# The first pair's keys turned on TensorE, and the 64 last positions in a transfer of their own

## The chip, the core and the metric

The kernel runs on one core of one Trainium2 chip. A time is the device time of one execution in microseconds (us). Where a median is given it is over several executions; the trace belongs to a single profiled one. Sizes are KB of 1024 bytes.

## What is computed

Attention with a decay in place of a softmax ("retention"), then two feed-forward layers. All data is float32.

```python
scores = q @ k.T / 8                      # 4 batches x 8 heads, 576 positions, 64 dims
ret    = scores * D                       # D[i,j] = gamma_h**(i-j) for i >= j, else 0
x      = (ret @ v) as (2304, 512)         # all heads side by side
h      = x @ w_in                         # 512 -> 2048
x      = (h * clip(h+3, 0, 6) / 6) @ w_out
h      = x @ w2_in                        # 512 -> 1024
solu   = h * softmax(h)
out    = (layernorm(solu) * g) @ w2_out   # 1024 -> 512
```

## The kernel before

**Pairs.** The 32 heads are taken two at a time, as 16 pairs (`pr`). The 576 positions of a head are four blocks of 128 and a last one of 64. `load_pair` brings four arrays for a pair: `rk` (k with the 64 dims of the two heads on the 128 partitions, one column per position), `rq` (q in the same way), `rv` (v with positions on the partitions) and `rn` (k again, now with positions, the keys, on the partitions). Before the change `rk`, `rq` and `rv` hold all 576 positions, with the last 64 at their end; `rn` holds 512. The first three pairs (`EARLY`) land in buffers that weights use later and are named `raw`; from the fourth pair on the buffers are `rk`, `rq`, `rv` and `rn` themselves.

**Work on a pair.** `scores` makes on TensorE (PE) the product of keys and queries inside each block (`s`), which ScalarE (ACT) copies out and GpSimd (POOL) masks (`st`). `short` does the same for the last 64 positions (`z`; VectorE, DVE, multiplies it by a mask into `st4`). `prep` scales v (`v`). `chunk_states` multiplies `rn` with `v` (`u`), and DVE sums it up from block to block (`state`). `values` adds st times v to the output `xp`, and the second half of `short` adds `st4` times v and state times q. `evac_x` takes xp out as `xa`, and splits it into the high and low parts of `x`. `places` makes a table once, with one PE product (`place`). From the pair with number 6 on, the first layer's products (`h`, six at a time) stand between the pairs.

**Order of the work.** For pair `pr` the loop puts on PE: scores of `pr`, values of `pr - 1`, short of both, states of `pr`. This order of PE is fixed by the text. The other engines and the DMA queue of SyncE (SP) get their order from `Plan`, which plays the program through with costs of its own and sorts each engine's queue by when an instruction is due. Its constants `HELD` (times at which it takes the transfers to stand still), `DMA_ONE` (the slowest single transfer) and the like change no instruction, only the order. Each queue then works strictly in that order. A transfer carries one of eight semaphores in turn, and the transfer eight places further down SP's queue waits for it: at most eight are under way, and the issue of the n-th tells that the one eight earlier has landed. ACT issues two small ones, which take two of these turns.

**The start.** Ahead of the first scores stand `N_WARM` products of a tile of zeros, `idle` (`warm`), which nobody reads. POOL makes the masks (`mask`).

Every recorded engine instruction has line 67, a helper's, so rows are told apart by the names of tiles. One float32 product shows as two records on PE, so eight products `s` are x16.

Of the kernel before, what the change touches and what calls it, by code (L numbers as in the profile page):

```python
# [109 lines left out]
class Plan:  # L110


    LOOK, HOP, DMA_US, DMA_KB, DMA_ONE = 0.8, 0.2, 2.2, 375.0, 150.0
    DEEP, PASSES, YIELD, GAP, KEEP = 3.0, 5, 0.3, 5.0, 1e9
    HELD = ((3.0, 1.4), (23.0, 0.3))

# [137 lines left out]
    def simulate(self, nexts, free, loose=False):  # L254
# [101 lines left out]
@with_exitstack  # L356
def retention_hardswish_solu_kernel(ctx, tc, kt, qt, kn, vt, w1, w2i, w2o, gln, decay, place, out):

# [536 lines left out]
    idle_b = known("x2e", idle)  # L895
    PA = {"rk": 3, "rq": 4, "rn": 3, "rv": 3, "v": 3, "st0": 2, "st1": 2, "state": 2, "st4": 2, "xa": 2}

# [6 lines left out]
    def at_x(c):  # L904

        return slice(128 + CHUNKS[c].start, 128 + CHUNKS[c].stop)

    def load_pair(pr):

        if pr >= NPAIR:  # L910
            return
        early = pr < EARLY
        tag = "wi" if pr < 2 else "g"
        rk, rq, rn, rv = (
            buf("g" if i == 3 else tag, shape, f"raw{pr}_{i}") if early else abuf(name, shape, f"{name}{pr}")
            for i, (name, shape) in enumerate((
                ("rk", [128, S]), ("rq", [128, S + 128]), ("rn", [128, 512]), ("rv", [128, 9, D]),
            ))
        )
        move(288, lambda: sy.dma_start(out=rk(), in_=kt[pr]), (), (rk,))  # L920
        n = S if early else S + 128
        move(n / 2, lambda: sy.dma_start(out=rq()[:, :n], in_=qt[pr][:, :n]), (), ((rq, 0),))
        move(288, lambda: sy.dma_start(out=rv(), in_=vt[pr]), (), (rv,))
        move(256, lambda: sy.dma_start(out=rn(), in_=kn[pr]), (), (rn,))
        for h in range(2 if early else 0):
            def go(e, h=h):
                o, i = rq()[HEADS[h], S:], rq()[HEADS[1 - h], CHUNKS[3]]
# [6 lines left out]
        raws[pr] = rk, rq, rn, rv  # L934

    def prep(pr):

        if pr >= NPAIR:
            return
        rv = raws[pr][3]  # L940
        v = vs[pr] = abuf("v", [128, 9, D], f"v{pr}")
        p = pr % NP
        for i, (c0, n, at) in enumerate(((0, 4, 2 * p), (4, 4, 2 * p + 1), (8, 1, H + NP + p))):
            def go(e, c0=c0, n=n, at=at):
                o, i = (x()[:, c0:c0 + n].rearrange("p c d -> p (c d)") for x in (v, rv))
# [5 lines left out]
            either(0.3 if n > 1 else 0.15, 0.5 if n > 1 else 0.33, go, (rv,), ((v, i),), "ACT").earliest = 5.6  # L951

    def scores(pr):

        sp = [pbuf(f"s{h}", [128, 512], f"s{pr}_{h}") for h in range(2)]
        st = sts[pr] = [abuf(f"st{h}", [128, 512], f"st{pr}_{h}") for h in range(2)]
        k, q, _, _ = raws[pr]
        wide = pr <= A_FROM
# [25 lines left out]
    def short(pr, now, old):  # L984
# [3 lines left out]
        if now:  # L988
            zp = pbuf("z", [128, 64], f"z{pr}")
            st4 = sts4[pr] = abuf("st4", [128, 64], f"st4{pr}")  # L990
            k, q, _, _ = raws[pr]
            reads, writes = [k, (q, 0)], [zp]
        first = pr > A_FROM
        if old:
            if first:
                xps[pr - 1] = pbuf("xp", [128, 1024], f"xp{pr - 1}")
            xp = xps[pr - 1]
            oq, v, state, ost4 = raws.pop(pr - 1)[1], vs[pr - 1], states.pop(pr - 1), sts4.pop(pr - 1)
            reads, writes = [*reads, oq, v, state, ost4], [*writes, xp]

        def go():
            for h in range(2):
                if old:
                    te.matmul(xp()[HEADS[h], at_x(4)], v()[HEADS[1 - h], 8], ost4()[HEADS[1 - h]], start=first, stop=False)
# [653 lines left out]
```

## Time and profile before

| | |
|---|---|
| median of 3 runs | 627.79 us (627.13 to 628.36) |
| the profiled execution | 627.86 us |
| its span, first to last instruction | 626.1 us |
| time outside the span | 1.76 us |
| PE busy | 620.6 us (99% of the span) |
| DVE, ACT, POOL busy | 464.2, 398.5, 313.5 us |
| DMA | 145.77 MB, mean 233 GB/s |

The page's slices show DMA engines busy at nine tenths or more from the start to some 80 us, at 391 to 408 GB/s after the first slice, and PE at 9 in nearly all. An engine's idle time is put down to what released it. "Busy" of PE counts an instruction from its start to a modelled end.

### The profile page before, as it was taken

What the parts mean: (1) busy time and instruction counts of PE and PEld (TensorE: products, weight loads), DVE (VectorE), ACT (ScalarE), POOL (GpSimd) and SP (SyncE); (2) the same over time, 40 slices, a digit from 0 to 9 for tenths busy, and PEclk for the clock granted to TensorE, in tenths of its full rate; (3) what the DMA queues carried; (4) which work ended last, traced back from release to release, by engine and by line L of the source; (5) the groups of instructions that cost most, each with busy time, mean ns of one, the idle gap of its engine ahead of it and who ended that gap; (6) DMA issues with size and microseconds to landing.
All of it is one profiled execution on the core that took longest, in us unless ns stands there. A gap on an engine that the chain in (4) does not pass through costs nothing.

```text
span 626.1 us, 11161 instructions
## 1 busy us (share of the span) xinstructions
PE 620.6 (99%) x3999; PEld 518.6 (83%) x3999; DVE 464.2 (74%) x830; ACT 398.5 (64%) x690; POOL 313.5 (50%) x315
## 2 busy tenths in 40 slices
PE   8999999999999999999999999999999999999997
PEld 5878888988888888888888888888988888888887
DVE  4887999876788785798689888552878868778740
ACT  5887867956667551567566665421676876877672
POOL 6764733304344402572054230542578998999453
PEclk9999999999999999999999999999999999999999
DMA  9999987859667695745998669966665553344441
GB/s 325 394 391 397 408 305 264 294 195 329 203 211 245 209 321 189 294 167 185 379 309 307 222 215 389 383 254 195 175 189 129 118 90 96 102 101 85 84 113 56
DMA packets 91914, 145.77 MB, mean 233 GB/s; under 512 B 43858, under 2 KB 49746, under 8 KB 91860
## 3 DMA queue, kind: packets, MB, share of 16 engines
q1 hardware_dynamic: 91712, 145.06, 69.6%
q8 instruction: 31, 0.51, 0.3%
q14 instruction: 23, 0.19, 0.1%
q10 hardware_dynamic: 148, 0.02, 0.0%
HBM read 92.36 MB, written 43.25 MB: 217 GB/s over the span
## 4 chain that ended last, share of the span: by engine, by line
PE 96%; DMA 3%; SPq 0%; issue 0%; ACT 0%
PE acc L67 29%; PE h L67 23%; PE o L67 16%; PE sd L67 6%; PE sc L67 6%; PE sa L67 6%; PE sb L67 3%; PE xp L67 3%; PE x L67 2%; PE s L67 2%; DMA rn<-in_kn_dram 1%; PE u L67 1%; DMA rk<-in_kt_dram 1%; DMA raw<-in_qt_dram 1%; SPq L67 0%; PE z L67 0%
## 5 line engine op out<-in xcount | busy, mean ns | idle before, releaser
L67 PE MATMUL acc<-g,w1l 128*128 128x512 f32 x624 | 154.1, 389 | 0.0
L67 PEld LDWEIGHTS acc<-g,w1l 128*128 128x128 f32 x624 | 117.1, 188 | 24.3
L67 PE MATMUL o<-w,lt 128*128 128x512 f32 (+1 forms) x456 | 103.0, 378 | 0.0
L67 PEld LDWEIGHTS o<-w,lt 128*128 128x128 f32 x456 | 82.4, 188 | 16.3 <-POOL lt L67 0.4
L67 POOL TENSOR_TENSOR lt<-lT,lt 128x512 fp32r<-128x512 f32 x36 | 61.2, 1719 | 13.4 <-ACT lt L67 13.2
L67 ACT ACTIVATE e<-h,stat 128x1024 f32<-128x1024 f32 x36 | 41.3, 1148 | 35.1 <-DVE stat L67 35.1
L67 PE MATMUL h<-w2t,xt 128*128 128x512 f32 x216 | 53.5, 389 | 0.0
L67 PEld LDWEIGHTS h<-w2t,xt 128*128 128x128 f32 x216 | 40.3, 188 | 8.2
L67 PE MATMUL h<-x,w 128*128 128x512 f32 (+1 forms) x216 | 45.8, 361 | 0.0
L67 PE MATMUL acc<-g,w 128*128 128x512 f32 (+1 forms) x216 | 43.5, 354 | 0.0
L67 PEld LDWEIGHTS acc<-g,w 128*128 128x128 f32 x216 | 36.5, 189 | 6.1
L67 PEld LDWEIGHTS h<-x,w 128*128 128x128 f32 x216 | 34.9, 189 | 7.0 <-issue 1.7
L67 PE MATMUL h<-w2b,xt 128*128 128x512 f32 x162 | 39.8, 390 | 0.0
L67 ACT ACTIVATE wz<-wraw 128x512 f32<-128x512 f32 x44 | 29.4, 668 | 12.9 <-DMA wraw<-in_w2o_dram 5.0
L67 POOL TENSOR_TENSOR g<-gf,g 128x512 fp32r<-128x512 f32 (+1 forms) x18 | 24.1, 1336 | 26.3 <-ACT g L67 26.2
L67 DVE CUSTOM_DVE_ANT_0 wz<-wz,wt 128x1024 uint16<-128x1024 uint16 x44 | 35.2, 801 | 2.3 <-ACT wt L67 1.1
L67 DVE TENSOR_SCALAR e<-h,stat 128x1024 f32<-128x1024 f32 x18 | 20.5, 1142 | 21.0 <-POOL stat L67 21.0
L67 PEld LDWEIGHTS h<-w2b,xt 128*128 128x128 f32 x162 | 30.2, 188 | 6.1
L67 ACT ACTIVATE wt<-wraw 128x512 int32<-128x512 uint32 x48 | 31.9, 664 | 3.4 <-DMA wraw<-in_w2o_dram 1.0
L67 DVE CUSTOM_DVE_ANT_0 h<-h,h 128x512 f32<-128x512 f32 x36 | 24.7, 685 | 11.7 <-PE h L67 4.7
L67 DVE SCALAR_TENSOR_TENSOR h<-h,e 128x1024 f32<-128x1024 f32 x18 | 28.1, 1563 | 7.0 <-ACT e L67 7.0
L67 ACT ACTIVATE g<-gf 128x512 fp32r<-128x512 f32 (+1 forms) x44 | 26.4, 600 | 10.2 <-DVE gf L67 8.9
(193 smaller groups left out, 1359.6 us busy)
## 6 DMA issues: line engine op xcount, KB each, us to landing
w1l<-w1s SPq DMA_DIRECT2D x34, 512.0 KB, 6.0
wraw<-in_w_dram SPq DMA_DIRECT2D x32, 512.0 KB, 5.7
w1s<-w1o SPq DMA_DIRECT2D x10, 512.0 KB, 4.5
x2l<-x2s SPq DMA_DIRECT2D x18, 256.0 KB, 5.9
x2f<-x2o SPq DMA_DIRECT2D x18, 256.0 KB, 5.1
x2r<-x2f SPq DMA_DIRECT2D x9, 512.0 KB, 4.6
rq<-in_qt_dram SPq DMA_DIRECT2D x13, 352.0 KB, 6.5
out_dram<-osb SPq DMA_DIRECT2D x17, 256.0 KB, 2.0
```

The source lines that it names most:

```text
L67: return lambda *args, **kw: self.keep(op(*args, **kw))
```

## The change

1. `load_pair` no longer loads the last 64 positions with `rk`, `rq` and `rv`. They come for all three in one new transfer `rt` (128 x 3 x 64, 96 KB), with four buffers. A pair's `rk`, `rv` are 256 KB in place of 288, `rq` is 320 in place of 352 (256 in place of 288 for the first three pairs). `short` and the third part of `prep` read `rt`.
2. The first pair's `rn` is not loaded. `flip` makes it: four products of a block of `rk` with a unit matrix `eye` put k on PE's output with the keys on the partitions, and one copy takes it out. `eye` is made on POOL with one fill and two masks. The buffer is one of the two of tag `gf`.
3. `short` of the first pair, so far right behind the first scores, stands behind the second pair's scores.
4. Six products `warm` in place of nine. `Plan` gets other times in `HELD`, and does not apply `DMA_ONE` to transfers begun in its first 2 us.

```diff
-N_WARM = 9
+N_WARM = 6
...
-    HELD = ((3.0, 1.4), (23.0, 0.3))
+    HELD = ((3.0, 0.4), (5.2, 0.4), (12.5, 0.6))
...
-                        o.end = max(dma, now + o.kb / self.DMA_ONE) + self.DMA_US
+                        o.end = max(dma, now + o.kb / self.DMA_ONE if now > self.FRESH else 0.0) + self.DMA_US
...
+    ge.memset(eye, 1.0)
+    for step in (1, -1):
+        ge.affine_select(
+            out=eye, in_=eye, compare_op=ALU.is_ge, fill=0.0, base=0, pattern=[[step, 128]], channel_multiplier=-step,
+        )
...
+    def flip(rk, rn):
...
+        def go():
+            for c in range(4):
+                te.matmul(kp()[:, CHUNKS[c]], rk()[:, CHUNKS[c]], eye, start=(c == 0), stop=(c == 3))
...
+        pl.op("PE", 0.95, go, (rk,), (kp,))
+        either(V_US, A_US, copy, (kp,), (rn,), "ACT")
...
-        move(288, lambda: sy.dma_start(out=rv(), in_=vt[pr]), (), (rv,))
-        move(256, lambda: sy.dma_start(out=rn(), in_=kn[pr]), (), (rn,))
+        move(256, lambda: sy.dma_start(out=rv(), in_=vt[pr]), (), (rv,))
+        rt = abuf("rt", [128, 3, 64], f"rt{pr}")
+        move(96, lambda: sy.dma_start(out=rt(), in_=short_rows[pr]), (), (rt,))
+        if pr:
+            move(256, lambda: sy.dma_start(out=rn(), in_=kn[pr]), (), (rn,))
+        else:
+            flip(rk, rn)
...
-                    te.matmul(zp()[HEADS[h]], k()[HEADS[h], CHUNKS[4]], q()[HEADS[h], CHUNKS[4]], start=True, stop=True)
+                    te.matmul(zp()[HEADS[h]], rt()[HEADS[h], 0], rt()[HEADS[h], 1], start=True, stop=True)
...
+        if pr == 1:
+            short(0, True, False)
         if past and not joined:
             values(pr - 1)
-        short(pr, more, past)
+        if pr:
+            short(pr, more, past)
```

PE, from the last `warm` to the first `xp`, before (repeated rows left out; the first number in a name is the pair, `raw0_0` to `raw0_3` are the first pair's rk, rq, rn and rv; DMAHW1 and so on are semaphores of transfers):

```order
L67 MATMUL warm_173<-idle_150 128x512
L67 MATMUL s0_0_197<-raw0_1_169,raw0_0_167 128x128 [waits DMAHW2_49,DMAHW1_49]
L67 MATMUL z0_209<-raw0_1_169,raw0_0_167 64x64 x2
L67 MATMUL place_214<-place_row_144 128x512 [waits DMAHW0_49]
L67 MATMUL u0_229<-v0_220,raw0_2_175 64x64 [waits DMAHW5_49,DVE_49]
L67 MATMUL s1_0_253<-raw1_1_182,raw1_0_179 128x128 [waits DMAHW7_49,DMAHW6_49,PE_49]
L67 MATMUL xp0_270<-st0_0_212,v0_220 64x128 [waits Pool_49]
```

The same piece of PE with the change:

```order
L67 MATMUL warm_181<-idle_151 128x512
L67 MATMUL flip_196<-eye_150,raw0_0_171 128x128 [waits DMAHW1_49,Pool_49]
L67 MATMUL s0_0_207<-raw0_1_173,raw0_0_171 128x128 [waits DMAHW2_49]
L67 MATMUL place_224<-place_row_144 128x512 [waits DMAHW0_49,PE_49]
L67 MATMUL u0_235<-v0_221,raw0_2_217 64x64 [waits DVE_49,Activation_49]
L67 MATMUL s1_0_250<-raw1_1_183,raw1_0_179 128x128 [waits DMAHW7_49,DMAHW6_49,Activation_49]
L67 MATMUL z0_275<-rt0_177 64x64 [waits DMAHW5_49]
L67 MATMUL xp0_279<-st0_0_229,v0_221 64x128 [waits Pool_49]
```

`flip` has come in ahead of the first scores, and `z0` has gone from behind `s0` to behind `s1`; `u0` waits for copies of DVE and ACT where it waited for a transfer. From here on PE's order is the same in both kernels but for the operands of `z` and of one product of `xp`.

SP's transfers around the fifth and sixth pair, before:

```order
L67 DMA wraw_338<-in_w1_dram 128x1024 [waits DMAHW4_49]
L67 DMA rv4_359<-in_vt_dram 128x576 [waits DMAHW5_49]
L67 DMA rq5_377<-in_qt_dram 128x704 [waits DMAHW6_49]
L67 DMA rn4_397<-in_kn_dram 128x512 [waits DMAHW7_49]
L67 DMA rk5_417<-in_kt_dram 128x576 [waits DMAHW0_49]
```

And with the change:

```order
L67 DMA wraw_353<-in_w1_dram 128x1024 [waits DMAHW7_49]
L67 DMA rv4_372<-in_vt_dram 128x512 [waits DMAHW0_49]
L67 DMA rn4_391<-in_kn_dram 128x512 [waits DMAHW1_49]
L67 DMA rq5_409<-in_qt_dram 128x640 [waits DMAHW2_49]
L67 DMA rt4_431<-in_rt_dram 128x192 [waits DMAHW3_49,PE_49,Activation_49]
L67 DMA rk5_435<-in_kt_dram 128x512 [waits DMAHW4_49]
```

`rn4` has gone ahead of `rq5`, and `rt4` stands between `rq5` and `rk5`. Added up over SP's queue from its first transfer, in KB of the transfers' sizes:

| up to and with | before: place, KB | with the change: place, KB |
|---|---|---|
| first pair's rq | 2nd, 576 | 2nd, 512 |
| second pair's rk | 5th, 1408 | 5th, 1120 |
| second pair's rq | 6th, 1696 | 6th, 1376 |
| first wraw | 19th, 5696 | 22nd, 5376 |
| rn4 | 22nd, 6592 | 24th, 5888 |
| rk5 | 23rd, 6880 | 27th, 6560 |

## Rows read from the trace of the kernel before

**Rows 1.** Busy time in stretches; the idle part of PE is length minus busy.
```profile
core 0: us, PE busy (x) PEld busy (x) DVE busy (x) ACT busy (x) POOL busy (x), PEclk, DMA share, GB/s
0.00:10.00 10.00, 7.97 (x69) 4.47 (x71) 3.35 (x13) 5.12 (x12) 5.17 (x21) 1.00 0.84 285
...
20.00:30.00 10.00, 9.66 (x208) 7.89 (x208) 8.58 (x25) 9.69 (x23) 7.33 (x10) 1.00 1.04 393
...
600.00:626.00 26.00, 22.96 (x123) 19.53 (x122) 6.04 (x11) 11.74 (x18) 10.31 (x9) 0.99 0.37 95
sum 626.00, PE 620.57 PEld 518.62 DVE 464.23 ACT 398.45 POOL 313.45; mean PE 44.33 PEld 37.04 DVE 33.16 ACT 28.46 POOL 22.39
```

**Rows 2.** Waits of PE: who, for whom, us in total, times, longest.
```profile
PE warm L67 <- DVE idle L440: 1.4, 1, 1.4
PE s L67 <- DMA raw<-in_qt_dram: 0.6, 1, 0.6
PE u L67 <- DMA rn<-in_kn_dram: 0.3, 1, 0.3
```

**Rows 3.** Timeline from 0 to 30 us, PE: start, us, what [idle before, releaser].
```profile
1.38 3.49 PE L67 MATMUL warm<-idle 128*128 128x512 bf16 x9 [1.38 <-DVE idle L440]
...
4.96 1.16 PE L67 MATMUL s<-raw,raw 64*128 64x128 f32 x16
...
6.05 0.33 PE L67 MATMUL z<-raw,raw 64*64 64x64 f32 x4
...
6.31 1.12 PE L67 MATMUL place<-place_row 2*128 2x512 f32 x2
...
7.36 0.69 PE L67 MATMUL u<-v,raw 128*64 128x64 f32 x16
...
8.61 1.16 PE L67 MATMUL s<-raw,raw 64*128 64x128 f32 x16 [0.56 <-DMA raw<-in_qt_dram]
...
9.70 1.29 PE L67 MATMUL xp<-st,v 128*64 128x128 f32 x17
```

**Rows 4.** Timeline from 3 to 5 us, weight loads of the last two warm products.
```profile
3.91 0.15 PEld L67 LDWEIGHTS <-idle 128*128 128x128 bf16 x1 [0.28 <-issue]
...
4.27 0.10 PEld L67 LDWEIGHTS <-idle 128*128 128x128 bf16 x1 [0.21 <-issue]
```

**Rows 5.** Timeline, issues on SP: the 9th, 13th to 17th transfer.
```profile
4.84 0.33 SPq L67 DMA_DIRECT2D raw<-in_kt_dram  x1
...
7.28 0.33 SPq L67 DMA_DIRECT2D rq<-in_qt_dram  x1
8.49 0.33 SPq L67 DMA_DIRECT2D rk<-in_kt_dram  x1
9.24 0.33 SPq L67 DMA_DIRECT2D rv<-in_vt_dram  x1
9.92 0.33 SPq L67 DMA_DIRECT2D rq<-in_qt_dram  x1
10.66 0.33 SPq L67 DMA_DIRECT2D rn<-in_kn_dram  x1
```

**Rows 6.** Tile raw up to 1.2 us: the first transfer, issued at 0.80, to its landing.
```profile
DMA to landing us min/median/max: 2.9/2.9/2.9
```

**Rows 7.** The chain that ended last: its last piece that is no work of PE.
```profile
14.48 7.55 DMA rn<-in_kn_dram
```

**Rows 8.** Timeline: the first weights, from their transfer to the first product h.
```profile
19.75 0.68 ACT L67 ACTIVATE wz<-wraw 128x512 f32<-128x512 f32 x1 [0.80 <-DMA wraw<-in_w_dram]
...
24.77 1.27 POOL L67 TENSOR_TENSOR w<-wz,w 128x512 fp32r<-128x512 f32 x1
...
26.31 1.66 PE L67 MATMUL h<-x,w 128*128 128x512 f32 x6
```

**Rows 9.** Timeline from 0 to 30 us: POOL's first work, and a DVE read of PE's output.
```profile
0.80 1.44 POOL L443 MEMSET mask<- 64x64 f32 x8 [0.29 <-POOLq L1647]
...
2.32 0.90 POOL L445 TENSOR_SCALAR_AFFINE_SELECT mask<-mask 64x256 f32<-64x256 f32 x2
...
11.65 0.76 DVE L67 TENSOR_TENSOR xa<-xp,tab_sb 128x576 f32<-128x576 f32 x1 [1.74 <-PE xp L67]
```

More of the change, by code (lines that the diff above doesn't have):

```diff
@@ L356, in retention_hardswish_solu_kernel @@
 @with_exitstack
-def retention_hardswish_solu_kernel(ctx, tc, kt, qt, kn, vt, w1, w2i, w2o, gln, decay, place, out):
+def retention_hardswish_solu_kernel(ctx, tc, kt, qt, kn, vt, short_rows, w1, w2i, w2o, gln, decay, place, out):
     nc = tc.nc
@@ L429, in retention_hardswish_solu_kernel @@
     mask4 = pa.tile([128, NP, 64], F32, name="mask4")
+    eye = pa.tile([128, 128], F32, name="eye")
     idle = p0.tile([128, 640], mybir.dt.bfloat16, tag="x2e", bufs=NE, name="idle")
@@ L895, in retention_hardswish_solu_kernel @@
     idle_b = known("x2e", idle)
-    PA = {"rk": 3, "rq": 4, "rn": 3, "rv": 3, "v": 3, "st0": 2, "st1": 2, "state": 2, "st4": 2, "xa": 2}
+    PA = {"rk": 3, "rq": 4, "rn": 3, "rv": 3, "rt": 4, "v": 3, "st0": 2, "st1": 2, "state": 2, "st4": 2, "xa": 2}
     def abuf(tag, shape, name):
@@ L906, in at_x, with copy @@
         return slice(128 + CHUNKS[c].start, 128 + CHUNKS[c].stop)
+    def flip(rk, rn):
+        kp = bank("flip", at=0)
+        def go():
+            for c in range(4):
+                te.matmul(kp()[:, CHUNKS[c]], rk()[:, CHUNKS[c]], eye, start=(c == 0), stop=(c == 3))
+        def copy(e):
+            if e is se:
+                se.activation(out=rn(), in_=kp(), func=ACTF.Copy)
+            else:
+                ve.tensor_copy(out=rn(), in_=kp())
+        pl.op("PE", 0.95, go, (rk,), (kp,))
+        either(V_US, A_US, copy, (kp,), (rn,), "ACT")
     def load_pair(pr):
@@ L914, in load_pair @@
         rk, rq, rn, rv = (
-            buf("g" if i == 3 else tag, shape, f"raw{pr}_{i}") if early else abuf(name, shape, f"{name}{pr}")
+            buf("gf" if not pr and i == 2 else "g" if i == 3 else tag, shape, f"raw{pr}_{i}") if early else abuf(name, shape, f"{name}{pr}")
             for i, (name, shape) in enumerate((
-                ("rk", [128, S]), ("rq", [128, S + 128]), ("rn", [128, 512]), ("rv", [128, 9, D]),
+                ("rk", [128, 512]), ("rq", [128, 640]), ("rn", [128, 512]), ("rv", [128, 8, D]),
             ))
         )
-        move(288, lambda: sy.dma_start(out=rk(), in_=kt[pr]), (), (rk,))
-        n = S if early else S + 128
+        move(256, lambda: sy.dma_start(out=rk(), in_=kt[pr]), (), (rk,))
+        n = 512 if early else 640
         move(n / 2, lambda: sy.dma_start(out=rq()[:, :n], in_=qt[pr][:, :n]), (), ((rq, 0),))
-        move(288, lambda: sy.dma_start(out=rv(), in_=vt[pr]), (), (rv,))
-        move(256, lambda: sy.dma_start(out=rn(), in_=kn[pr]), (), (rn,))
+        move(256, lambda: sy.dma_start(out=rv(), in_=vt[pr]), (), (rv,))
[3 more added lines that the diff above has]
+            move(256, lambda: sy.dma_start(out=rn(), in_=kn[pr]), (), (rn,))
+        else:
+            flip(rk, rn)
         for h in range(2 if early else 0):
             def go(e, h=h):
-                o, i = rq()[HEADS[h], S:], rq()[HEADS[1 - h], CHUNKS[3]]
+                o, i = rq()[HEADS[h], 512:], rq()[HEADS[1 - h], CHUNKS[3]]
                 if e is se:
@@ L944, in go @@
             def go(e, c0=c0, n=n, at=at):
-                o, i = (x()[:, c0:c0 + n].rearrange("p c d -> p (c d)") for x in (v, rv))
+                o = v()[:, c0:c0 + n].rearrange("p c d -> p (c d)")
+                i = rv()[:, c0:c0 + n].rearrange("p c d -> p (c d)") if n > 1 else rt()[:, 2]
                 if e is se:
@@ L949, in go @@
                     ve.tensor_scalar(out=o, in0=i, scalar1=decay_sb[:, at:at + 1], scalar2=None, op0=ALU.mult)
-            either(0.3 if n > 1 else 0.15, 0.5 if n > 1 else 0.33, go, (rv,), ((v, i),), "ACT").earliest = 5.6
+            either(0.3 if n > 1 else 0.15, 0.5 if n > 1 else 0.33, go, (rv if n > 1 else rt,), ((v, i),), "ACT").earliest = 5.6
     def scores(pr):
@@ L990, in short @@
             st4 = sts4[pr] = abuf("st4", [128, 64], f"st4{pr}")
[L991 to L992 removed]
+            rt = raws[pr][4]
+            reads, writes = [rt], [zp]
         first = pr > A_FROM
@@ L997, in short @@
             xp = xps[pr - 1]
-            oq, v, state, ost4 = raws.pop(pr - 1)[1], vs[pr - 1], states.pop(pr - 1), sts4.pop(pr - 1)
-            reads, writes = [*reads, oq, v, state, ost4], [*writes, xp]
+            (_, oq, _, _, ort), v, state, ost4 = raws.pop(pr - 1), vs[pr - 1], states.pop(pr - 1), sts4.pop(pr - 1)
+            reads, writes = [*reads, oq, ort, v, state, ost4], [*writes, xp]
         def go():
@@ L1602, in retention_hardswish_solu_kernel @@
     pb.release()
-_INS = ["kt", "qt", "kn", "vt", "w1", "w2i", "w2o", "gln", "decay", "place"]
+_INS = ["kt", "qt", "kn", "vt", "rt", "w1", "w2i", "w2o", "gln", "decay", "place"]
 def kernel(**inputs):
@@ L1614 @@
     kt, qt = (np.array(a.transpose(0, 2, 1).reshape(NPAIR, 2 * D, S)) for a in (k, q))
-    for a in (kt, qt):
-        a[:, :, 512:] = np.roll(a[:, :, 512:], D, axis=1)
-    qt = np.concatenate([qt, np.roll(qt[:, :, 384:512], D, axis=1)], axis=2)
+    rt = np.empty((NPAIR, 128, 3, 64), np.float32)
+    for i, a in enumerate((kt, qt)):
+        rt[:, :, i] = np.roll(a[:, :, 512:], D, axis=1)
+    kt, qt = kt[:, :, :512], np.concatenate([qt[:, :, :512], np.roll(qt[:, :, 384:512], D, axis=1)], axis=2)
     kn = k[:, :512].reshape(NPAIR, 2, 4, 128, D).transpose(0, 3, 2, 1, 4).reshape(NPAIR, 128, 512)
-    vt = np.empty((NPAIR, 128, 9, D), np.float32)
-    vt[:, :, :8] = v[:, :512].reshape(NPAIR, 2, 4, 128, D).transpose(0, 3, 1, 2, 4).reshape(NPAIR, 128, 8, D)
+    vt = v[:, :512].reshape(NPAIR, 2, 4, 128, D).transpose(0, 3, 1, 2, 4).reshape(NPAIR, 128, 8, D)
     for h in range(2):
-        vt[:, 64 * h:64 * h + 64, 8] = v[1 - h::2, 512:]
+        rt[:, 64 * h:64 * h + 64, 2] = v[1 - h::2, 512:]
     wi, wo, w2i, w2o = (
@@ L1644 @@
     place, decay = place.astype(np.float32), np.concatenate([over, step, last, np.roll(step, D, axis=0)], axis=1).astype(np.float32)
-    host = dict(kt=kt, qt=qt, kn=kn, vt=vt, w1=w1, w2i=w2i, w2o=w2o, gln=gln, decay=decay, place=place)
+    host = dict(kt=kt, qt=qt, kn=kn, vt=vt, rt=rt, w1=w1, w2i=w2i, w2o=w2o, gln=gln, decay=decay, place=place)
     nc = _bacc.Bacc("TRN2", target_bir_lowering=False, num_devices=1, dynamic_dma_scratch_size=1024)
```

12 lines of the change are left out of this document (6 added, 6 removed).

## Prediction

> **What bounds the kernel now.** First the busy time in stretches. PE's idle part of the whole span is 626.00 - 620.57 = 5.43 us; 2.03 us of it lie before 10 us, 0.34 us between 20 and 30 us and 3.04 us behind the last product [rows 1]. PE's order is the same in both kernels after the first 10 us, so a change in the start can only win what stands in these two early holes, or make new ones. Second, PE's waits: 1.4 us until the tile of zeros is there, 0.6 us of the second pair's scores for their q, and 0.3 us of a product u for a load of k by keys [rows 2]. Third, the timeline of the start shows what stands between them. Nine warm products from 1.38 fill the time until the first pair's q lands; then scores (4.96), z (6.05), place (6.31), u (7.36), and the second pair's scores at 8.61, 0.56 us after PE had come free [rows 3]. Fourth, the chain: its last piece that is not PE's is the load of rn4, issued at 14.48 and landed at 22.03 [rows 7]. From there to the last product PE sets the time.
>
> The transfers are the other side. Each issue on SP waits for an earlier landing. So the first pair's q landed at 4.84, the second pair's k at 7.28, its q at 8.49, and the next three at 9.24, 9.92 and 10.66 [rows 5]. In those last steps 256 KB took 0.68 us and 288 KB took 0.74 us, near 390 KB a us: the engines are full (share 1.04 [rows 1]), and what is loaded early decides when the second pair starts.
>
> Over 0.2% of the time (1.26 us) counts as a difference here.
>
> **The first transfers.** The first pair's k landed at 0.80 + 2.9 = 3.70 us [rows 6]; 32 KB less makes it about 3.6. The first q has 64 KB less before its end: 4.84 - 64/390 = 4.68. The second pair's q ends after 1376 KB in place of 1696. Before, 1408 KB had landed at 7.28, so it comes at 7.2; the step from 7.28 to 8.49 was 0.47 us longer than that of 0.74 [rows 5], and if that pause stays with this transfer, at 7.7.
>
> **flip.** Six warm products end at 1.38 + 6 x 0.43 = 3.94 (the last loads of weights are 0.43 us apart up to 3.91). `eye` costs POOL one fill and two masks ahead of or between the old fills: nine fills at 1.44/8 = 0.18 us and at most 0.45 us for a mask [rows 9] put its end at 0.80 + 1.62 + 0.90 = 3.32, before 3.94. So flip starts at 3.94, hidden until q lands. It is four float32 products of 128 columns: place needed 1.05 us for one of 512 columns (6.31 to 7.36 [rows 3]), so 1.05. The clock adds to it. The clock column shows 1.00 (2.4 GHz) for the whole stretch [rows 1], but 512 columns in 0.43 us are 1.2 columns a ns, the lower of the two levels. After PE had run the warm products back to back from 1.38, the last load of weights came 0.36 us behind the one before and took 0.10 in place of 0.15 us [rows 4]. So I put the rise at some 4.2 us; 0.26 us of flip at the lower level cost 0.13 more. Flip ends at 3.94 + 1.05 + 0.13 = 5.12. Bounds: it ends before q does (scores at 4.68, 0.28 earlier than now), or all of it runs at the lower level (2.1 us, scores at 6.04).
>
> **From the first scores to the second.** Scores 1.09 (4.96 to 6.05), place 1.05, u 0.64 (8.05 - 7.36 with its end) [rows 3]: 5.12 + 2.78 = 7.90. Two covers must hold. u now waits for DVE's copy of flip, some 0.76 us by the nearest read of PE's output [rows 9], done at about 6.0, and behind it on DVE for half of v, some 0.4 us more: 6.4, while PE is in place until 7.26. And the second q is there at 7.2 to 7.7. So PE runs through, and the second scores start at 7.90 in place of 8.61. Then z stands alone: 6.31 - 6.05 = 0.26. xp begins at 7.90 + 1.09 + 0.26 = 9.25 in place of 9.70: **0.45 us won**. Its st4 is multiplied on DVE behind the four sums of state now; that ends near 9.7, and xp needs it only after its first sixteen records, 1 us after 9.25. If this cover fails, xp waits at most the multiplication, 0.2 us.
>
> **The wait at 22 us.** rn4 stood behind 6592 KB and stands behind 5888: 704/390 = 1.8 us earlier, wanted 0.45 us earlier. **The 0.33 us go.** What is late next: rk5, which the sixth pair's scores need. 6560 KB are 32 less than rn4 had, so 22.03 - 0.08, plus five more transfers ahead of it than rn4 had (27 against 22). What a transfer costs beyond its bytes no row shows alone. Between the steps of 0.68 and 0.74 us, 32 KB cost 0.06, so 256 KB would cost 0.48, which leaves up to 0.20 a transfer; at 390 KB a us nothing is left. I take 0.05, near the second, as the share over 1 says that the engines hardly pause. That is 0.25 for five: rk5 at 22.2. The scores stood at 22.87, and are wanted at 22.87 - 0.45 - 0.33 = 22.09: **0.1 us is lost again** (0 to 0.9). The first weights also come closer: the chain from their transfer ran from 19.75 over ACT (97% busy between 20 and 30 [rows 1]) to POOL, which ended at 26.04, and h began at 26.31 [rows 8]. Their load ends 320 KB earlier and three transfers later in the count, 0.82 - 0.15 = 0.67 us sooner, about what PE has won. h waits 0 to 0.3 us; I take 0.
>
> **What is costed at nothing.** Loads of the later pairs carry the same bytes in five transfers in place of four; each lands well ahead of its use once h stands between the pairs, as PE has no idle time left there. rt4's issue waits for PE and ACT to be done with the first pair's, with rk5 and all later loads behind it on SP; both are done near 11 us, and its place comes after 14. The new times in the planner move stores and loads by a place or two all the way to 460 us; PE idled under 0.03 us in all of that, so there is room, and no row says where it ends.
>
> **Sum.** -0.45 - 0.33 + 0.1 = -0.68 us. The profiled execution took 627.86, 0.07 over the median: 627.2 us.
>
> A rule speaks against flip. The Trainium skill, "TensorE: Matmul & The Clock Gate", Part 4 (PE-mode transpose), says that a transpose by the identity in the transpose mode does not count as PE-busy in the way other products do. Flip is written as an ordinary product, and no run here shows such a case; by that rule the clock would rise later and the result would be the first rival's.
>
> **Rivals.**
> - *The clock rises later (slower).* Place: flip to the first u. In place of three harmless warm products, 1.18 us of real work now stands ahead of the scores, and 0.56 us of slack is gone, so lower-level time counts in full, at half price: each us by which the rise comes after 4.2 delays xp by 0.5. Even at 4.2 + 2 x (0.45 + 0.33) = 5.8 us; up 1.26 us at 8.3; a rise only behind the first u (11.5) costs 3.65 - 0.78 = 2.9 us: 630.7. For it: three warm products fewer, and a stop before flip if k is late. Against it: PE is as gapless as before, and the level changed between 3.91 and 4.27 [rows 4].
> - *The small transfers cost more than their bytes.* Then rk5 decides. If each costs the queue as much as its issue does (0.33 us [rows 5]), five cost 1.65: rk5 at 23.6, scores at 23.6 for 22.87: +0.7, 628.6. Against it: eight are under way at a time. The Trainium skill, "DMA: Bandwidth & Descriptors", Bandwidth, wants 1 MB a transfer and calls those under 64 KB descriptor-dominated. By its table (64 KB 0.95 us, 1 MB 6.15) 96 KB would take an estimated 1.1 us, 0.8 above their bytes, and rk5 would be 4 us late; the two steps above allow a quarter of that at most.
> - *The waits only move.* The early time is won, but rk5, or the first weights behind an ACT that is 97% busy, take it all back: 627.9.
> - *A new wait later.* Some reordered load or store makes PE wait between 76 and 460 us, 0.3 to 1.5 us: 628.2.
>
> **Chances.** Forecast 0.66, later clock 0.08, small transfers 0.08, waits that move 0.10, new wait 0.08. The forecast's own range is 0.3 to 1.2 us won: 626.7 to 627.6; the runs of before lie 1.2 us apart, so I widen it to 626.4 below, and to 628.6 above, which takes in three of the rivals. Faster by over 0.2% needs more than the two holes hold and so the scatter of runs: a fifth of the forecast, 0.13. Slower: 0.06 of the clock's chance, 0.03 each of small transfers and of the new wait: 0.12. The rest, 0.75, lies within.
>
> **What would show it.** Right: flip from about 3.9 to 5.1, first scores at 5.1, second scores at 7.9 with no idle time before them, xp near 9.25, no wait of u for rn4, rk5 at most 0.3 us late, first h near 25.6. Wrong: PE idle before flip or before the first u; scores of the first pair that take 2 us (clock); a wait of the second scores for q beyond 7.9; more than 0.5 us of waits between 20 and 30 us; any wait of PE over 0.1 us from 76 us on.

## The result, and the profile after

The changed kernel took 633.42 us (median of 6 runs, 631.37 to 636.58), the kernel before beside it 628.06 us (6 runs, 627.13 to 628.79). The ratio is 1.0089 with a 95% interval of 1.0071 to 1.0107: 5.4 us slower, where 0.7 us faster was forecast. The profiled execution has a span of 631.4 us, 5.3 more than before.

First, the busy time of the page of the changed kernel:

```profile
PE 623.0 (99%) x4004; PEld 520.1 (82%) x4004; DVE 463.7 (73%) x822; ACT 397.9 (63%) x690; POOL 330.9 (52%) x327
```

PE was busy for 620.6 us before and for 623.0 now, and its share of the span is still 99%: that share cannot show a loss of five microseconds. It went in a few small holes. So next the busy time in stretches, of the changed kernel:

```profile
core 0: us, PE busy (x) PEld busy (x) DVE busy (x) ACT busy (x) POOL busy (x), PEclk, DMA share, GB/s
10.00:20.00 10.00, 10.00 (x216) 8.48 (x212) 7.02 (x23) 7.46 (x18) 8.33 (x15) 1.00 1.04 382
20.00:40.00 20.00, 18.25 (x358) 14.51 (x358) 17.77 (x46) 15.88 (x36) 13.37 (x15) 1.00 1.04 366
40.00:60.00 20.00, 19.49 (x412) 15.82 (x403) 15.72 (x41) 15.31 (x32) 8.70 (x11) 1.00 0.99 343
60.00:80.00 20.00, 18.52 (x354) 14.36 (x347) 13.71 (x40) 14.96 (x31) 11.27 (x13) 1.00 1.03 398
```

and the same rows of the kernel before:

```profile
10.00:20.00 10.00, 10.00 (x216) 8.44 (x211) 6.24 (x19) 7.14 (x18) 7.41 (x13) 1.00 1.04 397
20.00:40.00 20.00, 19.66 (x410) 16.13 (x409) 16.88 (x45) 18.15 (x40) 14.56 (x19) 1.00 1.05 391
40.00:60.00 20.00, 20.00 (x388) 16.13 (x385) 16.18 (x48) 15.92 (x34) 10.30 (x13) 1.00 1.04 395
60.00:80.00 20.00, 20.00 (x338) 16.09 (x337) 18.01 (x41) 16.34 (x32) 12.58 (x13) 1.00 1.03 407
```

In the second column PE's 20 us between 20 and 40 us hold 18.25 us of work (19.66 before), those between 40 and 60 us 19.49 (20.00), those between 60 and 80 us 18.52 (20.00). The last column says with what: the transfers moved 366 and 343 GB/s where they had moved 391 and 395. The share of the DMA engines hardly tells it: 1.04 against 1.05 between 20 and 40 us, 0.99 against 1.04 in the next 20.

What PE waited for, in the changed kernel:

```profile
PE xp L67 <- DVE st L67: 1.7, 1, 1.7
PE xp L67 <- DVE xa L67: 1.5, 3, 0.8
PE warm L67 <- DVE idle L441: 1.4, 1, 1.4
PE u L67 <- issue: 0.5, 1, 0.5
```

Both waits of [rows 2] that the change was to remove are gone (for the second q and for rn4). In their place stand four waits for DVE, 3.2 us, and one of 0.5 us for which the profile shows no cause. The timeline of PE's start in the changed kernel:

```profile
1.38 2.74 PE L67 MATMUL warm<-idle 128*128 128x512 bf16 x6 [1.38 <-DVE idle L441]
3.91 1.80 PE L67 MATMUL flip<-eye,raw 128*128 128x128 f32 x8
5.64 1.16 PE L67 MATMUL s<-raw,raw 64*128 64x128 f32 x16
6.73 1.12 PE L67 MATMUL place<-place_row 2*128 2x512 f32 x2
7.78 0.69 PE L67 MATMUL u<-v,raw 128*64 128x64 f32 x16
8.40 1.16 PE L67 MATMUL s<-raw,raw 64*128 64x128 f32 x16
9.49 0.33 PE L67 MATMUL z<-rt 64*64 64x64 f32 x4
```

The start is nearly as laid out. Six `warm`, flip at 3.91, no idle time between flip and the first `xp`, second scores at 8.40 for 8.61 before, `xp` at 9.75 for 9.70 [rows 3]. Only flip took 1.73 us up to the first scores (1.80 with its modelled end), not 1.18. The loss is not here. Three of the waits further on, from PE's timeline (the number in brackets is the idle time before, and what ended it):

```profile
30.70 0.24 PE L67 MATMUL xp<-st,v 64*64 64x64 f32 x1 [1.67 <-DVE st L67]
...
69.58 0.27 PE L67 MATMUL xp<-st,v 64*64 64x64 f32 x1 [0.55 <-DVE xa L67]
...
79.28 0.27 PE L67 MATMUL xp<-st,v 64*64 64x64 f32 x2 [0.77 <-DVE xa L67]
```

and the work of DVE ahead of the first of them:

```profile
26.25 2.13 DVE L67 TENSOR_SCALAR v<-rv,decay_sb 128x256 f32<-128x256 f32 x2 [0.42 <-DMA rv<-in_vt_dram]
```

DVE had itself waited for a load, the seventh pair's rv, and multiplied it then, 1.07 us for each half, while the next outputs stood behind. But this load was not late: before, where ACT did the same work, it landed 0.4 us later.

```profile
26.69 1.15 ACT L67 ACTIVATE v<-rv,decay_sb 128x256 f32<-128x256 f32 x3 [0.23 <-DMA rv<-in_vt_dram]
```

So the first wait (1.67 us) comes from the planner's new order, which gave two scalings of v to DVE. The other two, and a fourth at 74.64 us, are waits for transfers at one remove. DVE could not take the next output out (`xa` has two buffers) until the store of an earlier one, `xd`, had landed. This is DVE ahead of the wait at 69.58:

```profile
68.77 0.76 DVE L67 TENSOR_TENSOR xa<-xp,tab_sb 128x576 f32<-128x576 f32 x1 [1.31 <-DMA xd<-xa]
```

These stores stand between the loads in SP's queue. DVE's waits for them from 20 to 80 us, in the changed kernel (first line) and in tiny_extra, an experiment below (second line):

```profile
DVE xa L67 <- DMA xd<-xa: 3.4, 5, 1.3
DVE xa L67 <- DMA xd<-xa: 8.7, 6, 2.7
```

The kernel before has none. All eight kernels with more transfers in SP's queue have 1.3 to 8.7 us of them, the ten others at most 0.7.

Aligned product by product, the two traces part like this: PE in the changed kernel is 0.05 us behind at the first `xp`, 0.02 ahead at 22 us, 1.9 behind at 29, 2.7 at 48, 3.8 at 71, 4.7 at 75, and 5.3 at 388 us. All but 0.6 us of the loss arises between 26 and 80 us. There the DMA engines are full before, and nearly full in the changed kernel.

### The profile page after: what moved, and what is told of

Its sections match the earlier page's. It is cut to its first block, busy times and chain, and to the rows that moved or that the text cites. A ratio compares the mean times of both kernels' runs of the same rounds, so it can differ in the third digit from the quotient of the medians.

```text
span 631.4 us, 11205 instructions
## 1 busy us (share of the span) xinstructions
PE 623.0 (99%) x4004; PEld 520.1 (82%) x4004; DVE 463.7 (73%) x822; ACT 397.9 (63%) x690; POOL 330.9 (52%) x327
## 4 chain that ended last, share of the span: by engine, by line
PE 85%; DMA 12%; DVE 1%; ACT 1%; SPq 0%; issue 0%; DVEq 0%; ACTq 0%
PE acc L67 28%; PE h L67 20%; PE o L67 16%; PE sd L67 5%; PE sa L67 5%; PE sc L67 5%; PE sb L67 3%; PE x L67 2%; DMA rt<-in_rt_dram 2%; DMA rq<-in_qt_dram 2%; DMA rv<-in_vt_dram 2%; DMA w2s<-ws 1%; DMA xd<-xa 1%; DMA rk<-in_kt_dram 1%; DMA wraw<-in_w_dram 1%; DMA rn<-in_kn_dram 1%
## 5 line engine op out<-in xcount | busy, mean ns | idle before, releaser
L67 POOL TENSOR_TENSOR w1f_s<-ws,w1f_s 128x512 fp32r<-128x512 f32 x18 | 25.9, 1444 | 55.6 <-ACT w1f_s L67 55.5
L67 DVE CUSTOM_DVE_ANT_0 wz<-wz,wt 128x1024 uint16<-128x1024 uint16 x44 | 38.2, 870 | 1.4
L67 DVE SCALAR_TENSOR_TENSOR h<-h,e 128x1024 f32<-128x1024 f32 x18 | 31.0, 1724 | 6.1 <-ACT e L67 6.1
L67 POOL TENSOR_TENSOR g<-gf,g 128x512 fp32r<-128x512 f32 x18 | 26.2, 1456 | 15.8 <-ACT g L67 15.7
```

The source lines that it names most:

```text
L67: return lambda *args, **kw: self.keep(op(*args, **kw))
```

## The experiments

Sixteen kernels ran. Every time is the median (lowest to highest), the ratio is against the kernel before on the same chip, and the last two columns are GB/s from 20 to 40 and from 40 to 60 us. The medians of before in the six sets were 628.0 to 628.1 us.

| kernel | us | ratio [95%] | 20-40 | 40-60 |
|---|---|---|---|---|
| before | 628.06 (627.13 to 628.79) | 1 | 391 | 395 |
| changed | 633.42 (631.37 to 636.58) | 1.0089 [1.0071, 1.0107] | 366 | 343 |
| flip_only | 628.95 (628.09 to 630.28) | 1.0016 [1.0006, 1.0025] | 384 | 373 |
| split_only | 633.90 (631.41 to 635.01) | 1.0086 [1.0063, 1.0110] | 372 | 372 |
| after_old_times | 633.80 (632.94 to 634.01) | 1.0091 [1.0074, 1.0108] | 365 | 362 |
| before_new_times | 630.41 (629.17 to 630.83) | 1.0035 [1.0024, 1.0046] | 394 | 385 |
| split_same_order | 633.04 (632.20 to 635.78) | 1.0088 [1.0062, 1.0113] | 346 | 316 |
| split_odd_pitch | 635.96 (634.20 to 637.74) | 1.0131 [1.0102, 1.0159] | 351 | 343 |
| rv_in_two | 633.48 (632.58 to 633.77) | 1.0085 [1.0070, 1.0100] | 377 | 316 |
| flip_old_times | 630.10 (628.61 to 630.39) | 1.0026 [1.0012, 1.0040] | 392 | 388 |
| tiny_extra | 632.93 (631.79 to 634.08) | 1.0068 [1.0051, 1.0086] | 366 | 316 |
| rv_two_pieces | 629.63 (628.53 to 632.78) | 1.0029 [1.0016, 1.0042] | 370 | 384 |
| rv_rn_joined | 628.62 (627.97 to 630.07) | 1.0011 [1.0002, 1.0021] | 403 | 364 |
| after_rv_rt_joined | 629.17 (628.50 to 629.99) | 1.0017 [1.0007, 1.0026] | 393 | 392 |
| tiny_on_pool | 633.12 (632.55 to 633.68) | 1.0072 [1.0050, 1.0095] | 365 | 360 |
| joined_old_times | 630.11 (629.20 to 632.28) | 1.0030 [1.0016, 1.0044] | 386 | 384 |
| tiny_13_sp | 632.15 (629.81 to 635.03) | 1.0054 [1.0031, 1.0076] | 370 | 327 |
| tiny_13_pool | 629.63 (629.21 to 631.01) | 1.0015 [1.0003, 1.0027] | 382 | 379 |

### Which part of the change

**flip_only** and **split_only** are the change without its other half; **after_old_times** and **before_new_times** set the planner's constants back, and put the new ones into the kernel before.

flip_only:
```diff
+        pl.op("PE", 0.95, go, (rk,), (kp,))
...
-N_WARM = 9
+N_WARM = 6
```


> Flip, the moved z of the first pair, six warm products and the new planner times; no transfer rt, all later loads as before. Transfers theory (the split makes the loads slower from 20 us on): 627.3 to 628.3 us, no PE wait over 0.5 us between 26 and 80 us. Planner theory (the new planner times put work into bad places): 630 to 634. Start theory (flip's own work and its clock): 630 or more, lost before 26 us.

split_only, and with the same one line the other way round after_old_times and before_new_times:
```diff
+        move(96, lambda: sy.dma_start(out=rt(), in_=short_rows[pr]), (), (rt,))
...
-    HELD = ((3.0, 0.4), (5.2, 0.4), (12.5, 0.6))
+    HELD = ((3.0, 1.4), (23.0, 0.3))
```


> The transfer rt for all pairs with 256 KB loads, nothing else: first k by keys loaded, z in its old place, nine warm products, old planner times. Transfers theory: 631 to 634 us, 340 to 375 GB/s between 20 and 60 us as in the changed kernel (before: 385 to 395). Planner and start theories: 627.5 to 629.

> The changed kernel with the old planner times (HELD, no FRESH). Transfers theory: 631 to 635 us, with waits in other places. Planner theory: 627 to 628.5, the wait of 1.7 us at 30.7 gone.

> The kernel before with the new planner times alone. Transfers theory: 627.5 to 629 us. Planner theory: 630 to 634.

The split alone costs as much as the whole change (633.90 against 633.42). The flip, with the planner's new times, costs 0.9 us where the prediction had it win. The planner's new times cost 2.4 us in the kernel before, but taking them out of the changed kernel wins nothing.

### Transfers, orders or addresses

The split does three things at once: one more transfer per pair, another order (the planner sees other sizes), and rows of 2048 bytes. **split_same_order** does the split with the planner led by the old sizes:
```diff
+        def two():
+            sy.dma_start(out=rv(), in_=vt[pr])
+            sy.dma_start(out=rt(), in_=short_rows[pr])
+        move(288, two, (), (rv, rt))
```


> The split of the change (last 64 positions of k, q and v in a load of 96 KB of their own, rk, rq and rv shorter, for all pairs) on the kernel before, but with the planner led by the old sizes: it sees the old loads (rv and rt are one planned load of 288 KB), so that every engine keeps the kernel before's order but for the first scalings of v1, which go to the other engine. No flip, nine warm products, old planner times. Theory A (one more transfer per pair costs time in a stretch where the transfers set the pace): 4 to 6 us slower than before, with PE's gaps between 26 and 80 us as in split_only. Theory B (the planner's new order of scalings and copies costs the time, above all v6's two scalings moved to DVE): within 1 us of before, as the order is before's. Halfway (2 to 3 us): both.

**split_odd_pitch** adds the old distances of the rows (`in_=kt[pr][:, :512]` and so on).

> As split_same_order, but the rows of kt, qt and vt in the chip's memory stay as far apart as before or farther (2304, 2816 and 2304 bytes, of which 2048, 2048 or 2560 and 2048 are read), so that no load has rows exactly 2048 bytes apart and back to back. Theory A (count of transfers): the same time as split_same_order. Theory C (packets take longer because rows of 2048 bytes lie at a pitch that falls on the same banks or channels; long packets summed to 3.6 us in the changed kernel, 0.8 before): back within 1 us of before, and the long packets back near 0.8 us.

**rv_in_two** leaves the data alone, and only cuts one load:
```diff
+            sy.dma_start(out=rv()[:, :5], in_=vt[pr][:, :5])
+            sy.dma_start(out=rv()[:, 5:], in_=vt[pr][:, 5:])
```


> The kernel before with one edit: rv is loaded by two transfers (five and four of its nine blocks of 64 values, 160 and 128 KB) in place of one, issued one behind the other where the one stood; same bytes, same order on every engine, row pitch as before, 128 packets more per pair. Theory A (one more transfer per pair costs time by itself): 4 us or more slower than before, gaps of PE between 26 and 80 us. Theories B (planner's order) and C (row pitch): within 0.7 us of before.

With the order of before, the split costs the same 5 us: theory B falls as the main cause. With the old distances it is worse, not better (636.0, also against A, which wanted no difference; why it lost 3 us more was not pursued), and theory C falls. The cut of rv alone costs 5.4 us, with the same bytes and, in the traces, the same order of work on DVE, ACT and POOL. So cutting one load per pair in two is enough. The DMA view from 20 to 60 us of rv_in_two:

```profile
DMA packets 8022, 13.85 MB, mean 346 GB/s; under 512 B 891, under 2 KB 3966, under 8 KB 8012
```

### A transfer or its packets

Cutting rv adds a transfer and 128 packets. **tiny_extra** adds the transfer and one packet:
```diff
             sy.dma_start(out=rv(), in_=vt[pr])
+            sy.dma_start(out=few, in_=vt[pr][0:1, 0:2].rearrange("p c d -> p (c d)"))
```


> The kernel before with one edit: behind each load of rv a transfer of 512 bytes (one packet: the first 128 values of the same rv) into a small tile that nothing reads. Hardly any bytes, one packet more per pair, but one transfer more among the eight that SP keeps under way. Theory W (SP issues a transfer only when the eighth before it has landed; a small one among the eight leaves fewer bytes under way, and engines run dry): 3 to 6 us slower than before, DMA share under 1.0 between 40 and 60 us. Theory D (packets and their descriptors cost the time): within 0.5 us of before.

**rv_two_pieces** adds the 128 packets and no transfer:
```diff
+    gap = np.zeros((NPAIR, 128, 2, 320), np.float32)
+    gap[:, :, :, :288] = vt.reshape(NPAIR, 128, 2, 288)
```


> The kernel before with one edit: each row of rv lies in two pieces of 1152 bytes with a gap of 128 bytes between them in the chip's memory, so that its one transfer of 288 KB has 256 packets in place of 128. As many transfers as before, the same bytes, 128 packets more per pair, as in rv_in_two. Theory W (number of transfers under way): within 0.7 us of before. Theory D (packets): about 5 us slower, as rv_in_two.

**rv_rn_joined** takes a transfer away:
```diff
+                both = pa.tile([128, 17, D], F32, tag="rvn", bufs=4, name=f"rvn{pr}")
+                sy.dma_start(out=both, in_=vt[pr])
```


> The kernel before with rv and rn of every pair from the fourth on side by side in the chip's memory and in one tile, loaded by one transfer of 544 KB where rv's stood: three transfers per pair in place of four, same bytes. Theory W: no slower than before, at best 0.3 to 0.5 us faster (before has no more idle time of PE than that between 10 and 80 us), DMA rate between 20 and 60 us at or above that of before (393, 390, 395 GB/s). Theory D: the same, as there are also fewer packets. If larger transfers make the first use of a load late (rv waits for rn's bytes, 0.66 us): 0.3 to 1 us slower.

**after_rv_rt_joined** puts the changed kernel's count back to four:
```diff
+                both = pa.tile([128, 11, D], F32, tag="rvt", bufs=4, name=f"rvt{pr}")
+                rv.tile, rt.tile = both[:, :8], both[:, 8:]
+                sy.dma_start(out=both, in_=vt[pr])
```


> The changed kernel with rv and rt side by side in one tile and one transfer of 352 KB for every pair from the fourth on (the first three pairs load them apart, as the change does): four transfers per pair again, all else as changed. Theory W (or D): most of the loss is gone, 627.5 to 629.5 us; what is left is the planner's order and the flip at the low clock. If it isn't the number of transfers that costs (the order of scalings, or k and q in rows of 2048 bytes): still 631 us or more.

The DMA view from 20 to 60 us (packets and rate; then loads with their count, size and median us from issue to landing) of before:

```profile
DMA packets 7337, 15.72 MB, mean 393 GB/s; under 512 B 813, under 2 KB 1325, under 8 KB 7326
...
rk<-in_kt_dram SPq DMA_DIRECT2D x10, 288.0 KB, 6.3
rv<-in_vt_dram SPq DMA_DIRECT2D x10, 288.0 KB, 6.1
rn<-in_kn_dram SPq DMA_DIRECT2D x10, 256.0 KB, 6.4
```

of the changed kernel:

```profile
DMA packets 7922, 14.19 MB, mean 355 GB/s; under 512 B 881, under 2 KB 2556, under 8 KB 7912
...
rk<-in_kt_dram SPq DMA_DIRECT2D x9, 256.0 KB, 5.8
rv<-in_vt_dram SPq DMA_DIRECT2D x9, 256.0 KB, 5.4
rn<-in_kn_dram SPq DMA_DIRECT2D x9, 256.0 KB, 5.7
rt<-in_rt_dram SPq DMA_DIRECT2D x9, 96.0 KB, 5.4
```

of after_rv_rt_joined:

```profile
DMA packets 7197, 15.71 MB, mean 393 GB/s; under 512 B 795, under 2 KB 1307, under 8 KB 7186
...
rvt<-in_vt_dram SPq DMA_DIRECT2D x9, 352.0 KB, 6.0
```

of tiny_extra:

```profile
DMA packets 6486, 13.63 MB, mean 341 GB/s; under 512 B 726, under 2 KB 1249, under 8 KB 6476
```

of rv_two_pieces:

```profile
DMA packets 8350, 15.09 MB, mean 377 GB/s; under 512 B 781, under 2 KB 3875, under 8 KB 8339
```

Sixteen transfers of 512 bytes cost 4.9 us, nearly all that the change cost, and bring the rate from 393 to 341 GB/s. rv_two_pieces has 8350 packets in the stretch, more than the changed kernel's 7922, and still moves 377 GB/s and costs 1.6 us. So the packets cost something, the transfer most. With rv and rt in one transfer the changed kernel is back at 393 GB/s and 629.17 us: 4.3 of its 5.4 us are gone. That run also got another order from the planner (ACT scales the seventh pair's v again), so a part of the 4.3 us may be the order's; tiny_extra and rv_in_two keep the order of DVE, ACT and POOL. Theory W foresaw these results but for the 1.6 us.

The arithmetic behind W: a pair is 1184 KB in both kernels. Eight transfers of four per pair hold 2 x 1184 = 2368 KB, eight of five per pair hold 8/5 x 1184 = 1894 KB. The landing time shrank much less (6.1 to 6.4 us before, 5.4 to 5.8 now). 2368 KB in 6.3 us are 385 GB/s, and 1894 KB in 5.6 us are 346. Both lie some 2% below the rates seen (393 and 355 GB/s), and the eight also hold weights of 512 KB.

The traces show the shortage. Issued on SP and not yet moved, read once each us from 20 to 60 us, were 1215 to 1995 KB before, 573 to 1922 in the changed kernel and 504 to 1562 in tiny_extra. Right at or behind the lowest points (51 and 41 us) only 9 and 8 packets were in progress at a time; in the kernel before no reading has fewer than 15. This is not the whole loss of rate. Between 20 and 40 us the changed kernel's engines were busy nearly as before (1.04) at 366 GB/s, so their packets took longer. Those of 4096 bytes took 192 ns on average from 20 to 60 us, 166 before, with medians of 159 and 162. Why some packets take so much longer is open.

Taking a transfer away raised the rate to 403 GB/s between 20 and 40 us, but PE had next to nothing left to win there, and from 40 to 60 us it was 364. Over both stretches its rate is 383, where theory W asked for 393 or more. rv_rn_joined is 0.6 us slower in the end, as its expectation had it if rv waits for the bytes of rn; that this is the cause was not tested. Its load took longer to land:

```profile
DMA packets 5725, 15.33 MB, mean 383 GB/s; under 512 B 637, under 2 KB 1149, under 8 KB 5714
...
rvn<-in_vt_dram SPq DMA_DIRECT2D x9, 544.0 KB, 7.5
```

### The eight, or a price of each transfer

The last rival (theory E): each transfer costs the DMA engines time wherever it comes from. **tiny_on_pool** issues the same sixteen from POOL, whose queue has a count of its own; **tiny_13_sp** and **tiny_13_pool** are a pair with thirteen each.
```diff
-            sy.dma_start(out=few, in_=vt[pr][0:1, 0:2].rearrange("p c d -> p (c d)"))
+            ge.dma_start(out=few, in_=vt[pr][0:1, 0:2].rearrange("p c d -> p (c d)"))
```


> tiny_extra with one word changed: the transfers of 512 bytes are issued by POOL, on a queue with a count of its own, and no longer stand among SP's eight. As many transfers and packets as in tiny_extra. Theory W (SP's eight): within 1 us of before (POOL spends some time on each issue), DMA rate between 40 and 60 us back near 395 GB/s. Theory E (each transfer, wherever it is issued, costs the 16 engines some 0.3 us for its start and its end): about 633 us, as tiny_extra.

It took 633.12 us, which by its time alone speaks for E. But its rate was 393 GB/s up to 30 us, and the loss came at one place, on DVE. This is the row of tiny_on_pool, and behind it the same product in the kernel before:

```profile
24.81 4.08 DVE L67 TENSOR_TENSOR x<-xa,x 128x64 fp32r<-128x64 f32 x1 [0.36 <-ACT x L67]
```

```profile
25.01 1.12 DVE L67 TENSOR_TENSOR x<-xa,x 128x64 fp32r<-128x64 f32 x1 [0.51 <-ACT x L67]
```

DVE's product of 64 columns took 4.08 us in place of 1.12, while POOL ran one instruction behind the other from 24.56 to 28.80, the first of them the issue (0.52 us). That speaks for a cost of issuing on POOL, not of the transfer. So the three pairs whose issue stood there were left out, on both queues.

> tiny_extra without the small transfers of the seventh to ninth pair: thirteen of 512 bytes, issued by SP behind rv. Only the partner of tiny_13_pool. Both theories: 632 to 633 us, of its 4.9 us over before some 4 (13/16).

> The same thirteen transfers of 512 bytes, issued by POOL, outside SP's eight. In tiny_on_pool the transfers kept their rate (395 and 393 GB/s from 10 to 30 us, as before), but one product on DVE took 4.08 us behind POOL's row of instructions between 24.8 and 28.9 us; the three pairs whose issue stood there are left out. Theory W (SP's eight): within 1 us of before, DMA rate of before in every stretch to 60 us. Theory E (a cost of each transfer on the DMA engines): as tiny_13_sp, 632 to 633 us.

The busy time in stretches of tiny_13_sp:

```profile
10.00:20.00 10.00, 10.00 (x216) 8.47 (x214) 5.88 (x19) 7.95 (x20) 7.68 (x16) 1.00 1.03 344
20.00:40.00 20.00, 18.37 (x348) 14.67 (x344) 14.92 (x43) 15.52 (x35) 13.04 (x16) 1.00 1.02 370
40.00:60.00 20.00, 19.14 (x381) 15.13 (x380) 15.26 (x42) 15.48 (x33) 10.79 (x13) 1.00 0.97 327
```

and of tiny_13_pool:

```profile
10.00:20.00 10.00, 9.58 (x208) 8.06 (x204) 6.97 (x19) 6.99 (x18) 9.21 (x18) 1.00 1.05 397
20.00:40.00 20.00, 19.79 (x410) 16.03 (x410) 16.81 (x43) 17.81 (x40) 14.89 (x20) 1.00 1.04 382
40.00:60.00 20.00, 19.36 (x387) 15.42 (x383) 16.33 (x46) 15.16 (x32) 13.35 (x19) 1.00 1.02 379
```

The same thirteen transfers leave the rate at 397 GB/s from 10 to 20 us when POOL issues them, and bring it down to 344 when SP does; 382 against 370 and 379 against 327 in the next stretches, 1.5 us against 4.1 us in the end (medians; both traces are of the slowest run of their kernel). POOL's landed after

```profile
few<-in_vt_dram POOLq DMA_DIRECT2D x7, 0.5 KB, 5.3
```

5.3 us, where loads of 256 to 352 KB took 6.2 to 6.6 us in the same stretch. SP's own small transfers can be read from the semaphores in the trace of tiny_extra: they landed 2.4 to 5.4 us after their issue, median 3.9, where its loads took 5.0 to 6.8 (medians of each kind). So a small transfer among SP's eight holds its place for more than half as long as a large one. Theory E falls as the main cause. It is not out altogether: W wanted at most 1 us and the rates of before, and 1.5 us were lost, at 382 and 379 GB/s for 391 and 395. POOL's issues at 0.5 us each are a cost that SP's did not have, and a transfer of 512 bytes went from POOL in pieces of 32 bytes (225 packets for the seven between 20 and 60 us), from SP in one piece. No run changed the number of places; that they are what counts, and not some other cost in SP's own queue, rests on this pair and on the KB not yet moved.

### What is left

**flip_old_times** and **joined_old_times** set the planner's old times into flip_only and after_rv_rt_joined, with the same line as after_old_times.

> The flip of the change alone with the planner's old times: first pair's k by keys made on PE, six warm products, z of the first pair behind the second pair's scores; loads as before, no split. If the planner's new times are what cost flip_only its 1 us (alone they cost 2.2 us), this is 627 to 628, at or a little below before. If the flip itself costs (it runs at the low clock, second scores 0.1 late), it stays at 628.5 to 629.5 as flip_only.

> after_rv_rt_joined with the planner's old times for the first transfers. If the planner's new times cost what is left of the loss (1.1 us over before): 627.5 to 628.3 us, no more than before's 628.0. If it is the flip's start at the low clock and the stricter order of the loads: 629 us or more.

Both lost another 1 us, so the new times are not what remains. Five kernels with four transfers per pair and an order of their own (flip_only, flip_old_times, before_new_times, after_rv_rt_joined, joined_old_times) lie 0.9 to 2.4 us above before. Each has some short waits of PE, 0.2 to 0.9 us each, for DVE or a load, and each at other places. No kernel was faster than before.

## Why the prediction was wrong

**The step that failed** is the first of "What is costed at nothing": "Loads of the later pairs carry the same bytes in five transfers in place of four; each lands well ahead of its use". Without the fifth transfer 4.3 us of the 5.4 are gone (after_rv_rt_joined, in another order). The sum priced five extra transfers up to rk5 at 0.05 us each, in one place at 22 us, and none after it. Spread over all sixteen pairs the price is 5.4 us/16 = 0.34 us by rv_in_two and 4.9/16 = 0.31 by tiny_extra, both in the kernel before with the order of DVE, ACT and POOL unchanged. That this is near the 0.33 us of the second rival is luck: the rival took the price as time of the issue on the queue, and for five transfers. The argument against it, "eight are under way at a time", was the mechanism itself. Eight places with fewer bytes in each are less work ahead of the engines.

**The cover** was read wrongly. PE had no idle time from 30 to 76 us, and the prediction took that for slack of the loads. The engines' share of 1.04 and 393 GB/s [rows 1] said that the transfers were at their limit too, with nothing to make up a loss. How far ahead they land was never read from a row. And the sentence names loads alone: much of what PE came to wait for, through DVE, were the stores `xd` that stand between them in the queue (waits of xp for xa: 1.5 us in the changed kernel, 3.6 in tiny_extra, 3.3 in rv_in_two).

**flip**: the sum said 1.18 us, 0.13 of it for the clock. It took 1.73 up to the first scores. Its records are 0.21 us apart up to 5.41, and those of the first scores 0.11 from 5.85 on, so flip ran at the lower level, 1.2 GHz, from end to end (the bounds of the prediction took that in). The first rival had a rise at 5.8 us eat up the gain, and at the start so it came: second scores at 8.40 in place of 7.90, xp 0.05 us late in place of 0.45 early.

**The waits at 8.6 and 22 us** went as said, also in flip_only (0.02 us ahead at 22.2). The loads came early enough there.

**Planner**: "no row says where it ends" was right to ask. The new times alone cost 2.4 us in the kernel before, so "a place or two" was not free. In the changed kernel the order gave DVE the two scalings ahead of the wait of 1.67 us; how much of the 5.4 us is the order's is not separated, as after_old_times took 633.80 with other waits. The fourth rival looked for a new wait between 76 and 460 us: 0.6 us came after 75, the rest ahead of it. The first h, expected near 25.6, began at 26.34 (26.31 before): with nothing won at the start, nothing reached it.

**The rule of the Trainium skill** beside the second rival, larger transfers, pointed the right way, and the estimate of 0.8 us a transfer from its table was more than twice the price. The Trainium skill, "DMA: Bandwidth & Descriptors", Bandwidth, asks for 1 MB. The traces agree with it in part: with 544 KB in one transfer the rate rose from 391 to 403 GB/s between 20 and 40 us, but fell from 395 to 364 in the next 20, and the kernel was no faster. No run shows a transfer of 1 MB. What showed the price were the places in the queue.

**Slips in the working**, none above 0.05 us: 1.38 + 6 x 0.43 is 3.96, not 3.94; u is 0.69 by the numbers named (8.05 - 7.36), not 0.64, and took 0.62 in the changed kernel; 393 GB/s are 384 KB a us, not 390.

**Left open**: which orders cost the last 1.1 us of after_rv_rt_joined, and why split_odd_pitch is slower than split_same_order.

## What to carry to other kernels

Where a queue keeps a fixed number of transfers under way and the DMA engines are full, count bytes in these places, not bytes in total. A small transfer between large ones holds its place for more than half as long as they do (3.9 us here); put its data beside a load that goes anyway. A store that shares the queue with loads is late with them: see which buffer it frees, and who waits for that. And an engine that never waits does not show that its loads have slack: look at the rate, and at the time from issue to landing against the time to use.

## What was not expected of the hardware

- 512 bytes behind each rv cost 4.9 us in sixteen pairs, as much as 96 KB there.
- The clock rose at different times in executions that begin alike. In the trace of before the ninth `warm` starts 0.22 us behind the eighth, at 4.49. In before_new_times, with the same nine, they are 0.43 us apart from the second up to the last at 4.76. flip's records are 0.21 us apart up to 5.41 in the changed kernel and up to 5.53 in flip_only. In all of them the granted clock's column says 1.00. A sum that lives on 0.5 us of this is not safe.
- One wait of 2.6 us cost 1.6 us more through the clock. These are the stretches of tiny_on_pool around it, with the granted clock as the third number from the end:

```profile
20.00:30.00 10.00, 8.79 (x172) 6.86 (x168) 9.15 (x18) 9.68 (x23) 8.68 (x14) 1.00 1.05 393
30.00:40.00 10.00, 8.56 (x151) 7.16 (x152) 6.29 (x21) 4.91 (x12) 5.58 (x9) 0.83 0.97 338
40.00:50.00 10.00, 10.00 (x191) 8.09 (x192) 9.21 (x24) 8.37 (x18) 7.33 (x10) 1.00 1.00 351
```

PE was 2.6 us behind when it began again at 31.4 us, 4.2 us at 35.5.
- DVE's 4.08 us behind POOL. The Trainium skill, "SBUF — State Buffer", section "SBUF: two separate sides", has it that a DVE operation with two inputs in SBUF and a POOL operation that reads SBUF lock each other out for whole instructions. The two rows (1.12 and 4.08 us for one form) agree that DVE can stand behind POOL. The trace goes further: DVE's product began at 24.81 and ended at 28.89, just behind the last of three POOL operations in a row (25.11 to 28.80).
